# Unit 1's x turned by DMA for three head pairs, and the first value weights loaded behind the value tiles

## The chip, the cores and the metric

The kernel runs on one core of one Trainium2 chip. The metric is the device time of one execution in microseconds (us), as the median of several runs.

## The reference

Four batches of eight heads, 768 positions of 64 dimensions. Each query attends to the keys less than 16 positions away and to 24 block summaries (the maximum of each block of 32 keys, the mean of its 32 values, with log 32 added to the score). The result, laid out as 3072 tokens of 512, goes through a gated feed-forward layer.

```
k_sum = k.reshape(B, H, nb, 32, D).max(axis=3)
v_sum = v.reshape(B, H, nb, 32, D).mean(axis=3)
s_l   = scale * q @ k^T, kept where |i - j| < 16
s_s   = scale * q @ k_sum^T + log(32)
x     = softmax([s_l, s_s]) @ [v, v_sum]            # as 3072 x 512
ffn   = (gelu(x @ w_gate) * (x @ w_val)) @ w_out    # d_ff = 1536
out   = x + sigmoid(x @ w_res) * ffn
```

## The kernel before, in words

The work is cut into eight units of 384 tokens, two for each batch. For a unit, four head pairs are scored (s_step: matmuls into s, Exp into P, a mask on DVE), weighted with the values (av_step: matmuls into ao, then DVE's reciprocal and product into xn, 128 tokens by 128 features for each of three sub-tiles), and turned into xT, features by tokens. The turning of one head pair is done either by xt_step (three TensorE transposes into PSUM tile xp, then a copy by ACT) or by xt_dma (one DMA transpose that SP issues). The tile xT is the moving operand of the gate and value matmuls g and vv (gv_mm): twelve blocks fo of 128 features, each with four matmuls for g and four for vv over the four head pairs ko. ACT takes Gelu of g, DVE multiplies it with vv into gvT. The output matmuls f (ffn_step) and the gate r (res_step) follow, and end_step (two DVE operations and a store by SP) for each of three sub-tiles.

The schedule is by hand: each engine executes its instructions in the order of the program. PE interleaves the output of unit u (first_out for u = 0, mid_out after) with the scores and values of unit u + 1. In first_out all four pairs are turned by xt_step; in mid_out all four by xt_dma.

Loads from DRAM are issued by POOL's queue, which also casts them to bf16; each of its transfers waits on a semaphore that is shared by turns with the one eight places earlier, so that about eight are outstanding. SP's queue issues the transposes, the stores and the copies within the value tiles (v_rims).

At the start, POOL issues the keys, the queries and value tiles 0 to 6 of 64 rows, the first chunk of w_gate and of w_val (256 features each), value tiles 7 to 11, then the other chunks by turns, the second half of the queries (q_sb), w_res, w_out, and later what batch 1 needs (k_sb, value tiles, q_nat). In the meantime PE fills its waits with matmuls on a dummy tile (keep_warm). The block means of the values for batch 0 come from 24 matmuls, two for each value tile (vsum_mm), into two tiles vs; they are copied by DVE and ACT to vblk, which the second half of av_first reads.

In unit 1, the keys of batch 1 are transposed by TensorE (turn_all, 64 transposes) at fo = 0 and placed into kW one pair at a time at fo = 0 to 3 (k_place: an ACT copy, then four DVE operations). At fo = 5 SP gets two DMA transposes of the queries (turn_q, q_nat to qT), PE twelve matmuls for the block means (vsum_grp), and POOL their transfers and copies (vsum_bc). The scores of unit 2 read kW and qT, its av_step the value tiles with the means in them.

Of the kernel before, what the change touches and what calls it, by code (L numbers as in the profile page):

```python
# [15 lines left out]
def kernel(  # L16
# [11 lines left out]
    nc = tc.nc  # L28
# [11 lines left out]
    NT = S // QT  # L40
# [4 lines left out]
    NP = H // 2  # L45
# [35 lines left out]
    w_gate = wpool.tile([128, KO, DFF], BF16, name="w_gate")  # L81
# [53 lines left out]
    with tc.manual_schedule():  # L135
# [20 lines left out]
        wg_src = moe_w_gate.rearrange("(ko ki) f -> ki ko f", ki=128)  # L156
        wv_src = moe_w_val.rearrange("(ko ki) f -> ki ko f", ki=128)

        def load_w(c):
            sl = slice(c * 256, (c + 1) * 256)  # L160
            nc.gpsimd.dma_start(out=w_gate[:, :, sl], in_=wg_src[:, :, sl])
            nc.gpsimd.dma_start(out=w_val[:, :, sl], in_=wv_src[:, :, sl])

        nc.vector.memset(warm[:], 0.0)
        nc.vector.memset(ident[:], 0.0)
# [18 lines left out]
            nc.gpsimd.affine_select(out=m, in_=m, compare_op=ALU.is_ge, fill=-240000.0, base=base,  # L184
                                    pattern=[[-sign, cols.stop - cols.start]], channel_multiplier=sign)
        v_loads(0, 6, 7)
        load_w(0)
        v_loads(0, 7, NT)
        kw_consts(0)
        own_keys(bmat, NT)  # L190
# [1 line left out]
        nc.vector.memset(vext[1][0:QT, :, :, D + 1:VP], 0.0)  # L192


        for c in range(1, 6):
            load_w(c)
            if c == 4:
                q_sb[1] = load_q(1, QJ)
        nc.gpsimd.dma_start(out=w_res[:], in_=moe_w_res.rearrange("(ko ki) f -> ki ko f", ki=128))
        wo_src = moe_w_out.rearrange("(fo ki) f -> ki fo f", ki=128)  # L200
        for c in range(3):
            sl = slice(c * 4, (c + 1) * 4)
# [38 lines left out]
        def k_place(b, hp, tp):  # L241
            nc.scalar.copy(kW[b % 2][:, :, hp, 0:QT].rearrange("d t (p j) -> d t p j", j=PJ),  # L242
                           tp.rearrange("d j (t p) -> d t p j", t=NT))
            k_blocks(b, hp)
            k_rims(b, slice(hp, hp + 1), nc.vector)
# [15 lines left out]
        def vsum_mm(b, vs, lo, hi):  # L261
            for t in range(lo, hi):
                for i in range(2):
                    nc.tensor.matmul(vs[i][96:128, 0:DM // 2], bmat[:, t, :],
                                     vext[b % 2][0:QT, t, 4 * i:4 * i + 4, 0:D],
                                     start=(t == 0), stop=(t == NT - 1))
# [36 lines left out]
        def s_step(u, hp, st, banks=None):  # L303
            if banks:
                s = [p.tile([128, 512], F32, tag=tag, name="s") for p, tag in banks]
            else:
                s2 = ps_s.tile([128, 2, 512], F32, tag="s", name="s")
                s = [s2[:, hh] for hh in range(2)]
            s_mm(u, hp, [x[:, 0:TU] for x in s])
            P = ppool.tile([128, 2, HT, QT], BF16, tag="P", name="P")  # L310
            if banks:
                for hh in range(2):
                    nc.scalar.activation(P[:, hh].rearrange("p t q -> p (t q)"), s[hh][:, 0:TU], AF.Exp,  # L313
                                         scale=scale, bias=bias_t[:])
            else:
                nc.scalar.activation(P.rearrange("p a t q -> p a (t q)"), s2[:, :, 0:TU], AF.Exp,  # L316
                                     scale=scale, bias=bias_t[:])
            if u or hp > 1:
                Pf = P.rearrange("p a t q -> p (a t) q")
                nc.vector.tensor_mul(Pf, Pf, maskt.unsqueeze(1).to_broadcast([128, 2 * HT, QT]))  # L320
            st["P", hp] = P
# [4 lines left out]
        def av_step(u, hp, st, pool=ps_o, tag="ao"):  # L326
            b, half = u // 2, u % 2
            P = st["P", hp]
            ao = pool.tile([128, NSUB, 2, D + 1], F32, tag=tag, name="ao")
            for sub in range(NSUB):  # L330
                for hh in range(2):
                    for e in range(2):
                        t = 2 * sub + e
                        nc.tensor.matmul(ao[64 * e:64 * e + 64, sub, hh, :], P[:, hh, t, :],  # L334
                                         vext[b % 2][:, half * HT + t, 2 * hp + hh, 0:D + 1],
                                         start=True, stop=True, skip_group_check=True)
            av_end(hp, st, ao)
# [18 lines left out]
        def xt_step(u, ko, st, pool, tag, copy=nc.vector.tensor_copy):  # L356
            xp = pool.tile([128, TU], BF16, tag=tag, name="xp")
            for sub in range(NSUB):
                nc.tensor.transpose(xp[:, sub * 128:(sub + 1) * 128],  # L359
                                    st["xn"][:, ko, sub, :], ident[:])  # L360
            copy(st["xT"][:, ko, :], xp[:])
# [115 lines left out]
        vsum_mm(0, vs, 0, 3)  # L477
        s_step(0, 2, st)
        s_step(0, 3, st, MM2)
        vsum_mm(0, vs, 3, 7)  # L480
        keep_warm(2)
        gvT = upool.tile([128, FO, TU], BF16, tag="gvT", name="gvT")
        ao = [ps_mm.tile([128, NSUB, 2, D + 1], F32, tag="mm", name="ao") for _ in range(NP)]
        for hp in range(3):
            av_first(hp, st, ao[hp], 0, BAND)
        vsum_mm(0, vs, 7, 10)
        av_first(3, st, ao[3], 0, BAND)
        vsum_mm(0, vs, 10, NT)
        nc.vector.tensor_copy(vblk[96:128, 0:H // 2, 0:D],
                              vs[0][96:128, 0:DM // 2].rearrange("p (h d) -> p h d", d=D))  # L490
        nc.scalar.copy(vblk[96:128, H // 2:H, 0:D],
# [49 lines left out]
        def first_out(u, st, gvT, nst):  # L541
            n = u + 1
            other = dict(pool=ps_t, tag="t")
            turn = dict(pool=ps_t, tag="t", copy=nc.scalar.copy)
            s_step(n, 0, nst)
            s_step(n, 1, nst, TO2)
            for sub in range(NSUB):
                res_step(st, sub)
            av_step(n, 0, nst)
            av_step(n, 1, nst, **other)  # L550
            s_step(n, 2, nst)
            for sub in range(NSUB):
                ffn_step(st, gvT, sub, 0, 4)
            xt_step(n, 0, nst, **turn)
            av_step(n, 2, nst)
            s_step(n, 3, nst)
            ffn_step(st, gvT, 0, 4, 8)
            ffn_step(st, gvT, 1, 4, 8)
            xt_step(n, 1, nst, **turn)
            ffn_step(st, gvT, 2, 4, 8)  # L560
            av_step(n, 3, nst)
            xt_step(n, 2, nst, **turn)
            ffn_step(st, gvT, 0, 8, FO)
            end_step(u, st, 0)
            ffn_step(st, gvT, 1, 8, FO)
            xt_step(n, 3, nst, **turn)
            ffn_step(st, gvT, 2, 8, FO)
            end_step(u, st, 1)
            end_step(u, st, 2)
# [40 lines left out]
        for u in range(NU):  # L610
            b, half = u // 2, u % 2
            nb = b + 1
            if half == 0 and nb == 1:
                k_sb[nb] = k_tile()
                load_k(nb, k_sb[nb], 0, 1)
                v_loads(nb)
                load_q_nat(nb)
            if u:
                gvT = upool.tile([128, FO, TU], BF16, tag="gvT", name="gvT")
            for fo in range(0 if u else 2, FO):  # L620
                if u > 1 and fo == 0:
                    fo_first(st, gvT)
                elif u and fo == FO - 2:
                    fo_last_two(st, gvT)
                elif u == 0 or fo < FO - 2:
                    fo_step(st, gvT, fo)
                if u == 0:
                    unit0_extras(fo)
                if u == 0 and fo == 9:
                    tq = turn_all(q_sb[1])  # L630
                if u == 0 and fo in (9, 10):
                    for hp in range(2 * fo - 18, 2 * fo - 16):
                        q_place(1, hp, tq[hp])
                if half == 0 and 1 < nb < B and fo == 0:
                    pool_after(st["xT"][0:1, KO - 1, 0:1])
                    k_nat = load_k_nat(nb)
                    v_loads(nb)
                if half == 0 and b and fo == 1:
                    v_rims(b, HT, NT)
                if half == 0 and 1 < nb < B and fo == 6:  # L640
                    turn_k(nb, k_nat)
                    k_rims(nb, slice(0, NP), nc.gpsimd)
                if half == 1 and nb < B:
                    if fo == 0:
                        v_rims(nb, 0, HT)
                        if nb > 1:
                            pool_after(st["xT"][0:1, KO - 1, 0:1])
                            load_q_nat(nb)
                    if fo == (5 if nb == 1 else 1):
                        turn_q(nb, 0)  # L650
                        turn_q(nb, 1)
                        vsum_grp(nb, ps_t, "t")
                        for i in range(2):
                            vsum_bc(nb, 3 * i, 3 * i + 3, nc.gpsimd)
                    if nb == 1:
                        if fo == 0:
                            tk = turn_all(k_sb[nb])
                        if fo < NP:
                            k_place(nb, fo, tk[fo])
                    elif 2 <= fo < 2 + NP:  # L660
                        k_blocks(nb, fo - 2)
            if u == NU - 1:
                last_out(u, st, gvT)
            else:
                nst = new_unit()
                (mid_out if u else first_out)(u, st, gvT, nst)
                st = nst
# [30 lines left out]
```

The softmax here doesn't subtract the row's maximum and nothing guards it: scores larger than these inputs give would overflow.

## Time and profile before

| what | value |
|---|---|
| median of 6 runs | 257.92 us (257.9 to 257.98) |
| profiled execution, its span | 257.9 us, 256.1 us |
| mean granted TensorE clock | 0.998 |
| PE, DVE, ACT, POOL busy | 248.3, 157.4, 127.3, 110.4 us |
| chain that ended last | PE 88%, DMA 5% |
| transposes of xn by PE (L359) | 24, 219 ns median |
| copies of xp by ACT (L361) | 8, 478 ns median |
| DMA transposes of xn (L364) | 24, landing 2.3 / 2.6 / 5.6 us (min, median, max) |
| first w_gate and w_val chunk issued | 10.59 and 11.34 us |
| first matmul of unit 1's gate | 53.18 us |

Times of instructions are microseconds from the first instruction. In the listings a line shows start, length, engine, source line, operation, the tiles written and read, and the count of instructions merged; in brackets stands the idle time before it and what ended it. PE's lengths overlap, as matmuls are pipelined. L359 is line 359 of the kernel.

### The profile page before, as it was taken

How to read it: one execution, taken by the hardware profiler on the slowest of the kernel's cores; microseconds unless marked ns; L12 is line 12 of the kernel's file. 1: busy time of each engine (PE TensorE's matmuls, PEld its weight loads, DVE VectorE, ACT ScalarE, POOL GpSimd, SP SyncE). 2: the span in 40 equal slices, each digit the busy share in tenths (PEclk: the TensorE clock that was granted, in tenths of full speed). 3: DMA queues.
4: the chain of work that ended last, by engine and by line, in shares of the span. 5: the costliest groups of instructions: out<-in, count | busy, mean ns of one | idle time of the engine just before them, and what ended most of it. 6: DMA issues, size and time to landing. Idle time of an engine off the chain costs nothing.

```text
span 256.1 us, 5810 instructions
## 1 busy us (share of the span) xinstructions
PE 248.3 (97%) x2279; PEld 139.0 (54%) x2304; DVE 157.4 (61%) x349; ACT 127.3 (50%) x213; POOL 110.4 (43%) x155
## 2 busy tenths in 40 slices
PE   7999999999999999999999999999999999999994
PEld 2555665565554565545654565546554665555543
DVE  5965776389467544767567544767567544854424
ACT  6667359356483337344492338344482338253320
POOL 8898443291334888255405987256404000000000
PEclk9999999999999999999999999999999999999999
DMA  5999999999903999989903999969903500240003
GB/s 81 178 156 179 197 203 207 183 167 180 137 3 77 179 112 141 130 138 173 131 5 93 181 105 148 120 128 167 140 15 80 134 0 3 49 139 0 0 3 123
DMA packets 98475, 29.34 MB, mean 115 GB/s; under 512 B 83592, under 2 KB 95312, under 8 KB 98352
## 3 DMA queue, kind: packets, MB, share of 16 engines
q0 software_dynamic: 68720, 14.76, 68.4%
q1 hardware_dynamic: 29728, 14.21, 26.1%
q8 instruction: 18, 0.29, 0.5%
q14 instruction: 9, 0.07, 0.2%
HBM read 29.36 MB, written 6.29 MB: 139 GB/s over the span
## 4 chain that ended last, share of the span: by engine, by line
PE 88%; DMA 5%; ACT 2%; POOL 2%; DVE 2%; issue 1%; POOLq 0%; DVEq 0%
PE g L374 25%; PE vv L374 24%; PE f L422 23%; PE r L412 7%; DMA q_sb<-in_q_dram 3%; PE ao L334 3%; PE s L298 2%; DMA vext<-in_v_dram 2%; PE tp L210 1%; PE vs L272 1%; DVE o L431 1%; DVE th L428 1%; POOL k_sb L88 1%; POOL vext L103 1%; PE xp L359 1%
## 5 line engine op out<-in xcount | busy, mean ns | idle before, releaser
L380 DVE TENSOR_TENSOR gvT<-ge,vv 128x384 bf16<-128x384 f32 x96 | 52.7, 552 | 50.8 <-PE vv L374 46.4
L379 ACT ACTIVATE ge<-g 128x384 f32<-128x384 f32 x96 | 47.0, 490 | 68.6 <-DVE gvT L380 38.1
L374 PE MATMUL g<-xT,w_gate 128*128 128x384 bf16 x384 | 78.8, 327 | 0.2
L374 PE MATMUL vv<-xT,w_val 128*128 128x384 bf16 x384 | 78.8, 327 | 0.0
L422 PE MATMUL f<-w_out,gvT 128*128 128x512 bf16 x262 | 62.7, 380 | 1.3 <-issue 1.0
L374 PEld LDWEIGHTS <-w_gate 128*128 128x128 bf16 x384 | 37.2, 98 | 26.5 <-issue 1.6
L374 PEld LDWEIGHTS <-w_val 128*128 128x128 bf16 x384 | 37.5, 98 | 24.8 <-issue 0.3
L422 PEld LDWEIGHTS <-gvT 128*128 128x128 bf16 x276 | 25.7, 98 | 29.2
L103 POOL DMA_DIRECT2D vext<-in_v_dram x48 | 33.5, 745 | 12.8 <-DMA w_out<-in_moe_w_out_dram 5.6
L415 ACT ACTIVATE th<-r 128x512 f32<-128x512 f32 x24 | 13.5, 606 | 27.5 <-PE r L412 27.5
L428 DVE SCALAR_TENSOR_TENSOR th<-th,f 128x512 f32<-128x512 f32 (+2 forms) x26 | 16.6, 640 | 14.5 <-PE f L422 14.5
L320 DVE TENSOR_TENSOR P<-P,maskt 128x768 bf16<-128x768 bf16 x30 | 16.8, 559 | 12.1 <-ACT P L316 6.6
L412 PE MATMUL r<-w_res,xT 128*128 128x512 bf16 x88 | 22.7, 380 | 0.4
L284 POOL COPY vext<-vsum 32x1536 bf16<-32x1536 bf16 x12 | 17.2, 1463 | 11.3 <-DMA vsum<-vpart 11.1
L431 DVE SCALAR_TENSOR_TENSOR o<-th,xn 128x512 f32<-128x512 f32 (+2 forms) x26 | 18.3, 702 | 0.9
L354 DVE TENSOR_TENSOR xn<-ao,rz 128x384 bf16<-128x384 f32 x32 | 17.8, 558 | 1.1
L316 ACT ACTIVATE P<-s,bias_t 128x768 bf16<-128x768 f32 x17 | 15.3, 902 | 4.3 <-PE s L298 4.1
L117 POOL DMA_DIRECT2D k_nat<-in_k_dram x24 | 16.4, 730 | 2.2 <-DMA k_nat<-in_k_dram 1.5
L123 POOL DMA_DIRECT2D q_nat<-in_q_dram x18 | 15.9, 924 | 0.7 <-issue 0.7
L313 ACT ACTIVATE P<-s,bias_t 128x384 bf16<-128x384 f32 x30 | 15.7, 580 | 0.0
L227 DVE TENSOR_REDUCE ks<-kW 128x24 bf16<-128x768 bf16 x16 | 15.1, 945 | 0.4 <-ACT kW L242 0.3
L412 PEld LDWEIGHTS <-xT 128*128 128x128 bf16 x96 | 8.8, 98 | 9.9
(82 smaller groups left out, 173.0 us busy)
## 6 DMA issues: line engine op xcount, KB each, us to landing
out_dram<-o SPq DMA_DIRECT2D x23, 256.0 KB, 2.2
vext<-in_v_dram POOLq DMA_DIRECT2D x48, 64.0 KB, 6.5
q_nat<-in_q_dram POOLq DMA_DIRECT2D x18, 128.0 KB, 7.4
w_gate<-in_moe_w_gate_dram POOLq DMA_DIRECT2D x6, 256.0 KB, 7.4
w_val<-in_moe_w_val_dram POOLq DMA_DIRECT2D x6, 256.0 KB, 8.0
w_out<-in_moe_w_out_dram POOLq DMA_DIRECT2D x3, 512.0 KB, 14.0
k_nat<-in_k_dram POOLq DMA_DIRECT2D x24, 64.0 KB, 4.5
vext<-vext SPq DMA_DIRECT2D x6, 144.0 KB, 5.3
```

Source lines behind the costliest of these rows:

```text
L103: nc.gpsimd.dma_start(out=vext[b % 2][0:QT, t, :, 0:D], in_=v[b, :, t * QT:(t + 1) * QT, :].rearrange("h p d -> p h d"))
L117: nc.gpsimd.dma_start(out=k_nat[:, t].rearrange("p (h d) -> p h d", d=D), in_=k[b, :, t * QT:(t + 1) * QT, :].rearrange("h p d -> p h d"))
L284: eng.tensor_copy(vext[b % 2][96:128, lo:hi, :, 0:D], src)
L320: nc.vector.tensor_mul(Pf, Pf, maskt.unsqueeze(1).to_broadcast([128, 2 * HT, QT]))
L354: nc.vector.tensor_mul(xn, ao[:, :, :, 0:D], rz.to_broadcast([128, NSUB, 2, D]))
L374: nc.tensor.matmul(ps[:, 0:TU], w[:, ko, fo * 128:(fo + 1) * 128], st["xT"][:, ko, :], start=(ko == 0), stop=(ko == KO - 1), skip_group_ch ...
L379: nc.scalar.activation(ge[:], g[:, 0:TU], AF.Gelu)
L380: nc.vector.tensor_mul(gvT[:, fo, :], ge[:], vv[:, 0:TU])
L412: nc.tensor.matmul(r[:], st["xT"][:, ko, ss], w_res[:, ko, :], start=(ko == 0), stop=(ko == KO - 1))
L422: nc.tensor.matmul(st["f", sub][:], gvT[:, fo, ss], w_out[:, fo, :], start=(fo == 0), stop=(fo == FO - 1), skip_group_check=True)
L428: nc.vector.scalar_tensor_tensor(th[:, cs], th[:, cs], 1.0, f[:, 0:n], ALU.add, ALU.mult)
L431: nc.vector.scalar_tensor_tensor(o.rearrange("p (k d) -> p k d", d=128), th[:, cs].rearrange("p (k d) -> p k d", d=128), 0.5, x, ALU.mult, ...
```

## The change

It has four parts. The function load_w loads one chunk of one weight matrix, and the first chunk of w_val is issued behind value tiles 7 to 11; the order behind it is as before. The block-mean matmuls of batch 0 are grouped by tiles 3 to 7, 8 to 10 and 11, in place of 3 to 6, 7 to 9 and 10 to 11. In first_out, pairs 0 to 2 of unit 1 are turned by xt_dma directly behind their av_step; pair 3 stays with xt_step. In unit 1, turn_all and the four k_place steps move from fo = 0 to 3 to fo = 1 to 4, and turn_q, vsum_grp and vsum_bc from fo = 5 to fo = 6.

```diff
--- before.py
+++ after.py
@@ -156,10 +156,9 @@
         wg_src = moe_w_gate.rearrange("(ko ki) f -> ki ko f", ki=128)
         wv_src = moe_w_val.rearrange("(ko ki) f -> ki ko f", ki=128)
 
-        def load_w(c):
+        def load_w(w, src, c):
             sl = slice(c * 256, (c + 1) * 256)
-            nc.gpsimd.dma_start(out=w_gate[:, :, sl], in_=wg_src[:, :, sl])
-            nc.gpsimd.dma_start(out=w_val[:, :, sl], in_=wv_src[:, :, sl])
+            nc.gpsimd.dma_start(out=w[:, :, sl], in_=src[:, :, sl])
 
         nc.vector.memset(warm[:], 0.0)
         nc.vector.memset(ident[:], 0.0)
@@ -184,7 +183,7 @@
             nc.gpsimd.affine_select(out=m, in_=m, compare_op=ALU.is_ge, fill=-240000.0, base=base,
                                     pattern=[[-sign, cols.stop - cols.start]], channel_multiplier=sign)
         v_loads(0, 6, 7)
-        load_w(0)
+        load_w(w_gate, wg_src, 0)
         v_loads(0, 7, NT)
         kw_consts(0)
         own_keys(bmat, NT)
@@ -192,8 +191,10 @@
         nc.vector.memset(vext[1][0:QT, :, :, D + 1:VP], 0.0)
 
 
-        for c in range(1, 6):
-            load_w(c)
+        for c in range(6):
+            if c:
+                load_w(w_gate, wg_src, c)
+            load_w(w_val, wv_src, c)
             if c == 4:
                 q_sb[1] = load_q(1, QJ)
         nc.gpsimd.dma_start(out=w_res[:], in_=moe_w_res.rearrange("(ko ki) f -> ki ko f", ki=128))
@@ -477,15 +478,15 @@
         vsum_mm(0, vs, 0, 3)
         s_step(0, 2, st)
         s_step(0, 3, st, MM2)
-        vsum_mm(0, vs, 3, 7)
+        vsum_mm(0, vs, 3, 8)
         keep_warm(2)
         gvT = upool.tile([128, FO, TU], BF16, tag="gvT", name="gvT")
         ao = [ps_mm.tile([128, NSUB, 2, D + 1], F32, tag="mm", name="ao") for _ in range(NP)]
         for hp in range(3):
             av_first(hp, st, ao[hp], 0, BAND)
-        vsum_mm(0, vs, 7, 10)
+        vsum_mm(0, vs, 8, 11)
         av_first(3, st, ao[3], 0, BAND)
-        vsum_mm(0, vs, 10, NT)
+        vsum_mm(0, vs, 11, NT)
         nc.vector.tensor_copy(vblk[96:128, 0:H // 2, 0:D],
                               vs[0][96:128, 0:DM // 2].rearrange("p (h d) -> p h d", d=D))
         nc.scalar.copy(vblk[96:128, H // 2:H, 0:D],
@@ -547,19 +548,19 @@
             for sub in range(NSUB):
                 res_step(st, sub)
             av_step(n, 0, nst)
+            xt_dma(0, nst)
             av_step(n, 1, nst, **other)
+            xt_dma(1, nst)
             s_step(n, 2, nst)
             for sub in range(NSUB):
                 ffn_step(st, gvT, sub, 0, 4)
-            xt_step(n, 0, nst, **turn)
             av_step(n, 2, nst)
+            xt_dma(2, nst)
             s_step(n, 3, nst)
             ffn_step(st, gvT, 0, 4, 8)
             ffn_step(st, gvT, 1, 4, 8)
-            xt_step(n, 1, nst, **turn)
             ffn_step(st, gvT, 2, 4, 8)
             av_step(n, 3, nst)
-            xt_step(n, 2, nst, **turn)
             ffn_step(st, gvT, 0, 8, FO)
             end_step(u, st, 0)
             ffn_step(st, gvT, 1, 8, FO)
@@ -646,17 +647,17 @@
                         if nb > 1:
                             pool_after(st["xT"][0:1, KO - 1, 0:1])
                             load_q_nat(nb)
-                    if fo == (5 if nb == 1 else 1):
+                    if fo == (6 if nb == 1 else 1):
                         turn_q(nb, 0)
                         turn_q(nb, 1)
                         vsum_grp(nb, ps_t, "t")
                         for i in range(2):
                             vsum_bc(nb, 3 * i, 3 * i + 3, nc.gpsimd)
                     if nb == 1:
-                        if fo == 0:
+                        if fo == 1:
                             tk = turn_all(k_sb[nb])
-                        if fo < NP:
-                            k_place(nb, fo, tk[fo])
+                        if 1 <= fo <= NP:
+                            k_place(nb, fo - 1, tk[fo - 1])
                     elif 2 <= fo < 2 + NP:
                         k_blocks(nb, fo - 2)
             if u == NU - 1:
```

## The prediction

> **What bounds the kernel now.** I read the page first. TensorE is busy for nearly the whole span at full clock, and the chain of work that ended last lies 88% on PE. DVE at 61% and ACT at 50% are not the limit over the whole.
>
> ```profile
> PE 248.3 (97%) x2279; PEld 139.0 (54%) x2304; DVE 157.4 (61%) x349; ACT 127.3 (50%) x213; POOL 110.4 (43%) x155
> ...
> PE   7999999999999999999999999999999999999994
> ...
> DMA  5999999999903999989903999969903500240003
> ```
>
> Two things follow. A matmul taken out of PE's stream shortens the run by its spacing. And the DMA row is full from about 6 to 70 us, so a transfer added there can become late. Next I read the chain in order of time, 12 to 20 us, where PE is not yet the chain:
>
> ```profile
> 11.35 0.74 POOL w_val L162
> 12.10 1.34 POOL vext L103 x2
> 13.44 4.52 DMA vext<-in_v_dram
> 17.96 0.04 issue
> 18.00 0.38 PE vs L264 x2
> 18.38 0.31 PE ao L346 x12
> 18.69 0.45 PE vs L264 x3
> 19.14 0.02 issue
> 19.17 0.45 DVE vblk L489
> ```
>
> Columns are start, length, what. The first value-weight load (w_val) is issued ahead of the value tiles. PE's sums (vs) wait for tile 9, landed at 17.96, and end with tile 11, landed at 18.82 by its semaphore. The copy to vblk, and all behind it, hangs on that. POOL's timeline gives the order of issue:
>
> ```profile
> 10.59 0.77 POOL L161 DMA_DIRECT2D w_gate<-in_moe_w_gate_dram  x1 [0.88 <-DMA q_sb<-in_q_dram]
> 11.34 0.75 POOL L162 DMA_DIRECT2D w_val<-in_moe_w_val_dram  x1
> 12.08 4.04 POOL L103 DMA_DIRECT2D vext<-in_v_dram  x5
> ```
>
> Then PE's timeline over the output of unit 0, where x of unit 1 is turned:
>
> ```profile
> 46.22 0.33 PE L359 MATMUL xp<-ident,xn 128*128 128x128 bf16 x3
> 46.48 0.38 PE L334 MATMUL ao<-vext,P 128*64 128x65 bf16 x12
> ...
> 48.81 0.33 PE L359 MATMUL xp<-ident,xn 128*128 128x128 bf16 x3
> 48.98 0.81 PE L422 MATMUL f<-w_out,gvT 128*128 128x512 bf16 x3
> ...
> 50.24 0.34 PE L359 MATMUL xp<-ident,xn 128*128 128x128 bf16 x3
> 50.42 1.89 PE L422 MATMUL f<-w_out,gvT 128*128 128x512 bf16 x8
> ```
>
> The lengths overlap, since matmuls are pipelined; cost is read from start to next start: 0.26, 0.17 and 0.18 us. Nothing waits there. Last, what a DMA transpose of the same shape takes in later units (instruction line, then landing of all):
>
> ```profile
> L364 SPq DMA_TRANSPOSE xT<-xn x24: 1178/1206/2400, 75.8 to 224.3; - x24
> ...
> DMA to landing us min/median/max: 2.3/2.6/5.6
> ```
>
> SP spends 1.2 us to issue one; it lands in 2.3 to 5.6 us.
>
> **What the Trainium skill says.** "TensorE: Matmul & The Clock Gate", Part 4, puts a 128x128 bf16 transpose at some 390 ns alone and 275 ns in a kernel. The trace disagrees for this stream: 219 ns each, and three cost 0.17 us of PE since they overlap, so I use 0.17. "DMA: Bandwidth & Descriptors", Anatomy of one DMA, has about 2 us of fixed cost per transfer; 2.3 us at least here agrees. The same page, Queues, rings and completion order, says that a DMA engine goes round its queues packet by packet, so SP's transposes should get turns beside POOL's loads. The trace agrees in part: with POOL's queue backed up, the transposes issued at 104.02 and 161.28 took 5.6 and 4.4 us, and their packets began only as that queue ran empty.
>
> **The change, part by part.**
>
> (1) *w_val behind the value tiles.* Tile 7 is issued at 11.34 in place of 12.08. Landings came at 14.35 (tile 6), 15.35 (w_gate), 16.67 (w_val), then every 0.44 us from 17.08 to 18.82: the queue is backed up, so a tile moves by w_val's share, 1.32 us. Tile 7 lands at 15.8, 8 to 11 at 16.2 to 17.5. If POOL's issue were the limit they would move only 0.74 us; I take 1.32, since even then issue to landing stays over 3 us. w_val itself lands where tile 11 did, 18.8; it is first used at 22.25. Cover 3 us. No load behind it moves.
>
> (2) *The sums regrouped, 3-8, 8-11, 11-12.* The same 24 matmuls. Tile 7's two (0.11 us each) enter the idle between 15.82 and 16.02, where PE waits for the Exp of pair 2 (ACT, 15.98): they run at 15.83, and the filler behind them starts 0.03 late. So: av_first of pairs 0 to 2 at 16.58 for 0.69; tiles 8-10 at 17.27, without waits, 0.12 + 5 x 0.11 + 0.09 into the next = 0.76; pair 3 at 18.03 for 0.31 (its mask is done at 17.51); tile 11 at 18.34, its second matmul 0.12 later. The last sum starts at 18.46 against 18.97: **-0.51 us**. Below, DVE's and ACT's copies, the table load and the xT copies follow it and hang on nothing else. The weights still come ahead of their use: the closest are w_val's last chunk (landed 35.79, used at 37.23, so 36.7 then) and w_res (38.30, used at 39.73, then 39.2), 0.9 us of cover.
>
> (3) *Three xt_steps out of PE.* Nine transposes: 0.17 + 0.17 + 0.18 = **-0.52 us** (of the first 0.26, 0.09 is a change of kind that stays). Three ACT copies of 478 ns go as well; ACT idles there (6.5 us waiting for xp over seven), so they are worth nothing.
>
> (4) *Three transposes onto SP.* SP is empty there until the stores at 52.93, so its 3 x 1.2 us hold nobody. xn of pairs 0, 1, 2 is ready at 43.67, 44.36 and 47.69, less 0.5 to 0.8 then: 43.2, 43.9, 46.9. The gate matmuls of unit 1 start at 53.18 - 1.03 = 52.15 and read pair 2 at 52.5. So the transposes have 8.9, some 7.5 and 5.5 us. With the worst landing seen, 5.6 us, the last costs 0.1 us. Bounds: 2.3 us (free) to a wait for POOL's queue to run dry (rival A). I take no stall. Their packets also take DMA time: 0.45 us each in later units, 1.35 together, out of a full queue; k_sb of batch 1 (landed 49.83) moves to at most 51.2 and is read at 54.7.
>
> (5) *turn_all and k_place one fo later, vsum_grp and turn_q at fo 6.* The same 64 transposes, 1.48 us. At fo 0 they stood between the first and second pair of gate and value tiles and covered DVE's three end_steps (51.49 to 55.55) and the Gelu table load (53.01 to 54.29). Without that cover, the value tile of fo 1 wants a bank at 52.15 + 3 x 0.65 = 54.1; the third end_step frees one at 54.83 - 1.03 = 53.8. 0.3 us to spare, so nothing; if the bank were another's, up to 0.4. vsum_grp then comes at 62.66 + 1.30 - 1.03 = 62.9, some 0.2 later, and so do POOL's vsum copies behind it.
>
> (6) *What is late next.* At the end of unit 1 PE comes 1.03 us earlier: s_step(2,0) at 71.33 - 1.03 = 70.3, av_step(2,0) at 73.4. Its qT was issued at 63.44, when q_nat's first half had landed, took 6.2 us and came at 69.66. That chain is held by DMA, not PE. The added 1.35 us of packets delays it by 0 (absorbed where POOL's issue was the limit, 51 to 54 us) to 1.35; I take 0.75, so 70.4. vsum's copies end at 72.98 + 0.2 to 0.7, wanted at 73.4. So **+0.2 us**, between 0 and 0.8.
>
> Sum: -0.51 - 0.52 + 0.2 = -0.8. The profiled execution took 257.9 (span 256.1 and 1.8 around it), 0.02 from the median of 257.92; so 257.1.
>
> **Rivals.** *A, slower: POOL's queue holds the transposes.* For: the DMA share is above 1.2 from 44 to 46 and 2.15 from 48.5 to 51.5, near the 2.37 at 104 to 106 where transposes stood still, and the backlog is longer here. Against: from 97.5 to 103 the kW transposes ran at 600 packets a us while POOL's got 80. It decides from a landing of pair 2 later than 53.5, 6.6 us after its issue, where the stall eats both gains. Held until the queue thins at 53.5, and then 1.35 for the packets and 0.8 to land, pair 2 comes at 55.6: stall 3.1, time 257.9 - 1.03 + 3.1 = 260.0.
>
> *B, absorbed: qT or vsum is the limit of unit 1.* With the full 1.35 us, or one of the pauses of transposes (packets of 1.7 us at 65.2), 0.7 us or more goes: 257.6, and 257.9 at the worst. For: qT's spare was 1.67 us, of which 1.03 is used. Against: the latency of 6.2 held such a pause already.
>
> *C, the value tiles don't move PE* (issue is the limit, or tile 7 holds av_first): then -0.52 + 0.2, so 257.6.
>
> **How the numbers follow.** Main case 0.56, its own range 256.7 to 257.3. B and C together 0.20, near 257.6. A 0.24, 258.5 to 260. About 0.2% (0.5 us) is what a measurement of this kernel tells from no change; so faster 0.56, same 0.20, slower 0.24. The range reaches from 256.6 (no loss, 0.2 more at the start) to 259.0, and leaves out A's long stalls and little else.
>
> **What would show it.** After: tile 11 lands near 17.5 and vblk's copy starts near 18.7 (against 19.17). Unit 1's first gate matmul starts near 52.1 and xT's DMA transposes of 44 to 47 us land by 52. PE between 52 and 54 without a gap means A is wrong; a gap ahead of g, released by the DMA xT<-xn, means A is right. A gap at s_step(2,0) near 70.3 released by qT is B. vblk near 19.2 is C. The prediction is wrong if pair 2's landing takes over 6.6 us.

## The result, and the profile after

The change makes the kernel slower by 0.6%: 259.53 us median (258.8 to 261.68, 36 runs) against 257.96 before (73 runs), ratio 1.0062 with the 95% interval 1.005 to 1.0074. Of the change 9 runs lie at 261.0 to 261.7, with a mean granted clock of 0.993 in place of 0.997 to 1.0, and of the kernel before 14 lie at 259.3 to 259.8; without them the medians are 259.46 and 257.93. The profiled execution took 259.2 us, span 257.5.

The page after: PE's busy time is the same, its share one point lower, and DMA's share of the chain has gone from 5% to 8% (the second and third lines are the chain that ended last, by engine and by line).

```profile
PE 248.2 (96%) x2270; PEld 138.4 (54%) x2295; DVE 156.9 (61%) x349; ACT 125.8 (49%) x210; POOL 110.7 (43%) x155
...
PE 83%; DMA 8%; POOL 3%; ACT 2%; DVE 1%; issue 1%; POOLq 0%; DVEq 0%
PE g L375 24%; PE vv L375 24%; PE f L423 21%; PE r L413 7%; DMA xT<-xn 3%; DMA q_sb<-in_q_dram 3%; PE ao L335 3%; PE s L299 2%; DMA w_val<-in_moe_w_val_dram 2%; POOL vext L103 1%; PE tp L211 1%; PE vs L273 1%; DVE o L432 1%; DVE th L429 1%; POOL w_gate L161 1%
```

The new entry is xT<-xn. PE's timeline around unit 1's first gate matmuls, before,

```profile
53.18 0.81 PE L374 MATMUL g<-xT,w_gate 128*128 128x384 bf16 x4
```

and after, shows where it sits:

```profile
51.27 0.33 PE L360 MATMUL xp<-ident,xn 128*128 128x128 bf16 x3
51.44 1.03 PE L423 MATMUL f<-w_out,gvT 128*128 128x512 bf16 x4
52.30 0.33 PE L375 MATMUL g<-xT,w_gate 128*128 128x384 bf16 x1
53.35 0.32 PE L375 MATMUL g<-xT,w_gate 128*128 128x384 bf16 x1 [0.72 <-DMA xT<-xn]
54.63 0.49 PE L375 MATMUL g<-xT,w_gate 128*128 128x384 bf16 x2 [0.96 <-DMA xT<-xn]
```

The matmul on pair 0 starts at 52.30, 0.88 us ahead of before (53.18). The matmul on pair 1 waits for its transpose, then the one on pair 2 does. Without waits these would be 0.16 us apart, so 1.05 + 1.28 - 0.33 = 2.0 us is lost, and unit 1 goes on 2.01 - 0.88 = 1.13 us behind before. That difference is the same at the first gate matmul of each later unit, 2 to 7. The other 0.3 us of the span's 1.4 lie behind the last DVE operation, at the last stores (that operation ends at 253.40 of 256.1 before and at 254.53 of 257.5 after).

The transposes themselves, in the view of the tile xT:

```profile
L365 SPq DMA_TRANSPOSE xT<-xn x27: 1179/1205/2119, 43.3 to 224.2; - x27
...
DMA to landing us min/median/max: 2.3/2.7/8.6
```

Three more than before, and the slowest landing is 8.6 us in place of 5.6. Pairs 0, 1 and 2, issued at 43.32, 44.68 and 47.17, took 7.95, 8.63 and 7.42 us and landed at 51.27, 53.31 and 54.59.

The start did what it should. POOL's timeline after:

```profile
10.58 0.77 POOL L161 DMA_DIRECT2D w_gate<-in_moe_w_gate_dram  x1 [0.89 <-DMA q_sb<-in_q_dram]
11.34 3.67 POOL L103 DMA_DIRECT2D vext<-in_v_dram  x5
14.99 1.07 POOL L161 DMA_DIRECT2D w_val<-in_moe_w_val_dram  x1
```

Tile 11 lands at 17.57 (18.82 before), DVE's copy to vblk starts at 18.80 (19.17), and unit 0's first gate matmul at 21.72 (22.09). DVE's timeline after:

```profile
18.80 0.43 DVE L490 CAST vblk<-vs 32x256 bf16<-32x256 f32 x1 [1.22 <-PE vs L265]
```

### The profile page after: what moved, and what is told of

It is laid out like the page before. It is cut to its first block, busy times and chain, and to the rows that moved or that the text cites. A ratio compares the mean times of both kernels' runs of the same rounds, so it can differ in the third digit from the quotient of the medians.

```text
span 257.5 us, 5797 instructions
## 1 busy us (share of the span) xinstructions
PE 248.2 (96%) x2270; PEld 138.4 (54%) x2295; DVE 156.9 (61%) x349; ACT 125.8 (49%) x210; POOL 110.7 (43%) x155
## 4 chain that ended last, share of the span: by engine, by line
PE 83%; DMA 8%; POOL 3%; ACT 2%; DVE 1%; issue 1%; POOLq 0%; DVEq 0%
PE g L375 24%; PE vv L375 24%; PE f L423 21%; PE r L413 7%; DMA xT<-xn 3%; DMA q_sb<-in_q_dram 3%; PE ao L335 3%; PE s L299 2%; DMA w_val<-in_moe_w_val_dram 2%; POOL vext L103 1%; PE tp L211 1%; PE vs L273 1%; DVE o L432 1%; DVE th L429 1%; POOL w_gate L161 1%
## 5 line engine op out<-in xcount | busy, mean ns | idle before, releaser
L103 POOL DMA_DIRECT2D vext<-in_v_dram x48 | 32.9, 739 | 15.5 <-DMA w_out<-in_moe_w_out_dram 5.7
L123 POOL DMA_DIRECT2D q_nat<-in_q_dram x18 | 15.8, 912 | 0.7 <-issue 0.7
```

The costliest lines, as they stand in the source:

```text
L103: nc.gpsimd.dma_start(out=vext[b % 2][0:QT, t, :, 0:D], in_=v[b, :, t * QT:(t + 1) * QT, :].rearrange("h p d -> p h d"))
```

## The experiments

Two theories stood first. Theory Q: the loss is PE's wait for xT, and xT is late because its packets share the DMA engines with POOL's backlog. Rival L: the loads that the change delays cost by themselves. A third, T, was that a transpose is slow of its own accord at this place. The edits are cut to the lines that matter, with ... where lines are left out. Those of the start, the turning, the later turn_all and the better version are shown against the kernel before or, for the last, against the start alone; the others against the change.

**The start alone.** All turning stays on PE.

```diff
-        load_w(0)
+        load_w(w_gate, wg_src, 0)
         v_loads(0, 7, NT)
...
-        for c in range(1, 6):
-            load_w(c)
+        for c in range(6):
+            if c:
+                load_w(w_gate, wg_src, c)
+            load_w(w_val, wv_src, c)
...
-        vsum_mm(0, vs, 3, 7)
+        vsum_mm(0, vs, 3, 8)
...
```

> Only the start of the change: w_val's first chunk behind all value tiles and the block means regrouped; all four pairs of unit 1 turned by PE as before. Theory Q (the whole loss is the wait for xT, whose packets share the DMA engines with POOL's loads): the start's gain seen in the trace after, 0.37 us at unit 0's first gate matmul, is kept to the end: 257.9 - 0.4 = 257.5. Rival L (the loads behind w_val came 0.7 us later in the trace after, and that costs by itself at w_res, w_out or q_nat): 257.9 or more.

Measured: 257.52 us (257.4 to 258.27), ratio 0.9972 (0.996 to 0.9983). PE is 0.38 us ahead at unit 0 and 0.39 at every later unit. The start's gain is real and kept; all of the loss is in the rest of the change.

**The turning alone.** The old start, with everything else of the change.

```diff
+            xt_dma(0, nst)
...
-            xt_step(n, 0, nst, **turn)
...
```

> Only the turning by DMA with the later turn_all, on the old start. Theory Q: when pair 2 lands is set by POOL's queue and not by PE, so it lands at 54.6 again and the time is that of the whole change, 259.2 to 259.5, though PE starts 0.4 us later. Rival T (a transpose is slow by itself at this place, so its landing follows its issue): all is 0.4 us later than in the whole change, 259.6 to 259.9. If the turning is innocent: 257.4.

Measured: 260.03 us (259.15 to 262.15), ratio 1.0081 (1.0052 to 1.011). The median looks like rival T's, but five of the ten runs, the profiled one among them, had a granted clock of 0.993 (260.41 to 262.15); the other five took 259.15 to 259.65, in theory Q's range. The landings took 7.56, 7.40 and 7.55 us. Each transpose was issued 0.4 us later than in the change. Pair 0 landed at 51.27 as there, pair 1 at 52.47, 0.8 us earlier, and only pair 2 later, at 55.12; but in other runs whose transposes stood beside the same loads pair 2 landed anywhere from 54.58 to 55.35. So this run doesn't tell Q from T. It showed something else, told below.

**Spare transposes.** PE turns pairs 0 to 2 again, and the same three DMA transposes go to a tile without a reader.

```diff
-            xt_dma(0, nst)
+            xt_spare(0, nst)
...
+            xt_step(n, 0, nst, **turn)
...
```

> The whole change, but PE turns pairs 0 to 2 as before, and the three DMA transposes go to a tile that nobody reads. Theory Q: the cost is PE's wait for the landing alone; without a reader the time is 257.9 - 0.4 = 257.5, up to 0.3 more for loads that come late. Rival L (the 1.35 us of added packets make k_sb, the value tiles and qT late, and that costs): 258.2 or more, with a gap at vs of unit 1 or at the scores of unit 2. Theory Q expects the spare transposes to land 7 to 9 us after their issue also here.

Measured: 258.24 us (257.73 to 258.47), ratio 0.999 (0.9973 to 1.0008). The spare transposes took 8.25, 7.60 and 7.18 us, so the delay is not one of xT. PE ran 0.33 us ahead through all of unit 1, without a gap at the gate matmuls. Without the reader the 2 us are gone: the cost is the wait. But 0.56 us was lost at unit 2: 0.22 where the scores waited for qT (landed 71.18), and 0.33 at the value matmuls, behind a mask on DVE that took 1.35 us. So rival L seems to exist as well, with a smaller sum, hidden in the change because PE is late there anyway. A run below shows that about half of the 0.56 comes without any DMA transpose.

**POOL's loads of batch 1 held back** until pair 2 has landed.

```diff
+            pool_after(nst["xT"][0:1, 2, 0:1])
+            k_sb[1] = k_tile()
+            load_k(1, k_sb[1], 0, 1)
+            v_loads(1)
+            load_q_nat(1)
...
-            if half == 0 and nb == 1:
-                k_sb[nb] = k_tile()
-                load_k(nb, k_sb[nb], 0, 1)
-                v_loads(nb)
-                load_q_nat(nb)
```

> The whole change, with POOL's loads of batch 1 (keys, values, queries) held back until pair 2's transpose has landed, so that only w_out's loads stand beside the transposes. Theory Q: pair 0 lands 4 to 5 us after its issue (w_out until 46.8), pair 2 in under 3.5 us, and unit 1's first gate matmuls have no gap; the loads that come 15 us later then cost 3 us or more at turn_all and at the scores of unit 2 (time 260.5 to 264). Rival T: pairs 0 to 2 land 7 to 9 us after their issue as in the whole change, gap 1.7 us at the first gate matmuls.

Measured: 264.7 us (two runs), somewhat above the expected range. PE waits 3.25 us for the late keys in one piece, and 6.8 us at half clock follow. But the landings took 4.04, 3.10 and 2.33 us, and PE's timeline of this kernel has no gap at unit 1's first gate matmuls:

```profile
51.62 1.03 PE L423 MATMUL f<-w_out,gvT 128*128 128x512 bf16 x4
52.49 0.81 PE L375 MATMUL g<-xT,w_gate 128*128 128x384 bf16 x4
53.14 0.81 PE L375 MATMUL vv<-xT,w_val 128*128 128x384 bf16 x4
```

T falls: the same transposes at the same place are quicker without batch 1's loads in POOL's queue, and pair 2, which finds that queue empty, is as quick as any. Theory Q stands.

**How the queues share.** The DMA view counts packets of POOL's queue (q0) and SP's (q1) in a stretch. Of the change, 47.5 to 49 us, while batch 1's keys come in packets of 1 KB:

```profile
q0 software_dynamic: 230, 0.23, 91.7%
q1 hardware_dynamic: 230, 0.06, 29.7%
```

One for one. At that rate a transpose of 384 packets takes 384 / 230 x 1.5 = 2.5 us; in the kernel with the loads held back pair 2's packets, with no others beside them, took 0.6 (48.53 to 49.13). It is one for one too in 49.5 to 50.5 us, when most of POOL's packets are already the value tiles' of 128 B:

```profile
q0 software_dynamic: 312, 0.09, 84.7%
q1 hardware_dynamic: 318, 0.07, 67.5%
```

In 51 to 51.75 us the counts are far apart:

```profile
q0 software_dynamic: 736, 0.09, 279.5%
q1 hardware_dynamic: 49, 0.01, 11.8%
```

This is no share between two full queues. By count, 735 of the 768 data packets of pairs 0 and 1 had started by 51.0 and the last of them at 51.49; pair 2's first started at 51.58. SP's queue had little left to send there.

Two parts of the delay are not explained by the turns. The first packets start at 47.25, 3.9 us after the first issue, where with idle queues they start after about 1.2 (1.17 for the transpose of 133.1 us before). This time is 3.9 to 4.0 us in all nine traces with DMA transposes here and batch 1's keys queued, and 1.6 in the one with the keys held back. And pair 1 landed at 53.31, 1.8 us after the last of those 768 packets had started. What sets these two times is not shown.

To see whether the one for one is of packets or of bytes, the keys were loaded in 512 B rows:

```diff
-                load_k(nb, k_sb[nb], 0, 1)
+                for j in range(0, PJ, 4):
+                    nc.gpsimd.dma_start(
+                        out=k_sb[nb][:, :, j:j + 4].rearrange("p h j d -> p h (j d)"),
+                        in_=k[nb].rearrange("h (p j) d -> p h j d", j=PJ)[:, :, j:j + 4].rearrange(
+                            "p h j d -> p h (j d)"))
```

> The whole change, with batch 1's keys loaded by two transfers with 512 byte rows in place of one with 1 KB rows. Theory Q in its packet form (one of SP's packets for one of POOL's): the transposes go at 250 to 300 packets a us beside the keys in place of 150, pair 0 lands at 50 or before in place of 51.3 and pair 2 before 53.7. Byte form (the shares are of bytes or fixed): 150 packets a us and 51.3 as before.

Measured: 259.38 us, ratio 1.0053 (1.0035 to 1.0071). The DMA view of this kernel, 48 to 49.5 us:

```profile
q0 software_dynamic: 371, 0.19, 90.1%
q1 hardware_dynamic: 358, 0.09, 45.7%
```

Still about one for one, now at 240 packets a us: it is packets that alternate. Pair 0 landed at 50.47, 0.8 us earlier, though it was issued 0.45 later. Pair 2 landed at 54.72 all the same, past the 53.7 expected; the next run shows what held it.

**Only the value and query loads held back,** the keys left in place.

```diff
+            pool_after(nst["xT"][0:1, 2, 0:1])
+            v_loads(1)
+            load_q_nat(1)
...
                 load_k(nb, k_sb[nb], 0, 1)
-                v_loads(nb)
-                load_q_nat(nb)
```

> The whole change, with POOL's value and query loads of batch 1 held back until pair 2's transpose has landed; the keys stay where they are. Theory Q (the DMA engines alternate between SP's packets and POOL's): beside the keys' 1 KB packets the transposes go at 150 packets a us as before, pair 0 lands at 51.3; when the keys end near 51.4 the rest goes at 800 a us, so pairs 1 and 2 land at 52 to 53 in place of 53.3 and 54.6, and the gap at unit 1's first gate matmuls falls from 1.8 to at most 0.7 us. The loads then come some 3 us later or more and cost 2 us or more at the scores of unit 2: 260 to 262. If the value tiles' small packets hold nothing, pair 2 still lands after 54.

Measured: 260.32 us (258.78 to 262.13, three runs). Pairs 0, 1 and 2 landed at 51.69, 51.96 and 52.29, and the gap is gone:

```profile
52.27 0.81 PE L375 MATMUL g<-xT,w_gate 128*128 128x384 bf16 x4
```

So the keys make the transposes slow (with them held back too, pair 0 had taken 4.04 us in place of 8.40), and the value tiles hold the last two beyond 52.3. At unit 2 PE then waited 2.38 us for qT, whose loads came late.

**Filler in the wait.** Nine dummy matmuls on PE ahead of unit 1's gate.

```diff
             ffn_step(st, gvT, 2, 8, FO)
+            keep_warm(9)
             end_step(u, st, 1)
```

> The whole change, with nine 128x512 matmuls on the dummy tile (0.216 us each) on PE ahead of unit 1's gate matmuls, inside the wait for xT. If the runs of the change at 261 us come from TensorE's clock, which was granted at half for 3.4 us behind a gap of 2.1 us in the run with the turning alone: no run above 260.2, median 259.2 to 259.6. If they come from elsewhere: a quarter of the runs at 261 as before. If PE's wait is not what costs: all 1.9 us slower, 261.4.

Measured: 259.79 us (259.16 to 260.17), not the 261.4 that 1.9 us more work (nine of 0.216 us) would cost outside a wait. Pair 2's matmul starts at 54.63, to the hundredth as in the change, and in both 0.04 us behind its landing: the wait is set by the landing alone. Repeated beside the change itself:

> The kernel with filler matmuls in the wait once more, beside the change itself on the same chip. Clock theory (a gap of over 2 us in PE's matmuls costs a stretch at half clock): no run above 260.3 here, some at 260.8 to 261.7 of the change. Otherwise both have such runs.

> The whole change once more, unaltered, beside the filler kernel: 258.8 to 259.9 for most runs, and a quarter of them at 261.

Measured: filler 259.40 us (259.09 to 260.0, 10 runs), the change 259.45 (258.94 to 259.71, 9 runs). So the filler changes the time by nothing that these runs can tell. On the clock, which the expectation asked about, the repeat does not decide: no run with filler came above 260.2, but here none of the change did either. Pair 2 landed at 55.35 and 54.85 in these two profiled runs, so its landing varies by some 0.8 us from run to run.

**Start and later turn_all,** no DMA transpose.

```diff
-                        if fo == 0:
+                        if fo == 1:
                             tk = turn_all(k_sb[nb])
...
-                    if fo == (5 if nb == 1 else 1):
+                    if fo == (6 if nb == 1 else 1):
...
```

> The start of the change and the later turn_all, k_place, turn_q and vsum_grp, with all pairs turned by PE. It parts the 0.56 us that the kernel with spare transposes lost at the scores and values of unit 2. If the packets of the transposes made qT and the value sums late there: 257.5, as the start alone (257.52), and PE 0.39 us ahead of before at unit 2. If the later vsum_grp did it: 257.8 to 258.1, and the first values of unit 2 wait for POOL's copy.

Measured: 257.83 us (257.44 to 258.27), 0.31 above the start alone. PE is 0.39 ahead to the end of unit 1 and 0.12 from unit 2 on. So the move of part 5 has a price when PE is early, and of the 0.56 us that the kernel with spare transposes lost, some 0.27 needs no transpose. The time is as expected for the later vsum_grp; what waited was a mask on DVE. DVE's timeline of this kernel:

```profile
72.47 2.02 DVE L321 TENSOR_TENSOR P<-P,maskt 128x768 bf16<-128x768 bf16 x2 [0.81 <-ACT P L317]
```

and of the start alone:

```profile
72.48 0.62 DVE L321 TENSOR_TENSOR P<-P,maskt 128x768 bf16<-128x768 bf16 x1 [0.81 <-ACT P L317]
73.43 0.56 DVE L321 TENSOR_TENSOR P<-P,maskt 128x768 bf16<-128x768 bf16 x1 [0.32 <-ACT P L314]
```

The first mask operation took 1.55 us in place of 0.62. POOL's timeline of the shifted kernel has the reason:

```profile
70.74 2.87 POOL L285 COPY vext<-vsum 32x1536 bf16<-32x1536 bf16 x2 [3.31 <-DMA vsum<-vpart]
```

POOL's copies of the block means run to 73.61, 0.9 us later than in the start alone (72.70), and so beside the mask operations of unit 2. The Trainium skill, "SBUF — State Buffer", SBUF: two separate sides, says that GpSimd and a DVE operation with two SBUF inputs take turns on a shared port pair, each holding it for its whole instruction. The trace agrees: the mask ended at 74.02, 0.41 us behind POOL's second copy. The same 0.40 to 0.41 us stands behind the copy's end in the start alone (copy 72.70, mask 73.10), with spare transposes (74.44 and 74.84, a mask of 1.35 us) and with the filler (74.78 and 75.19). It wasn't tried with the copies on another engine.

**A better version.** The start, and pair 0 alone by DMA; turn_all where it was.

```diff
             av_step(n, 0, nst)
+            xt_dma(0, nst)
...
-            xt_step(n, 0, nst, **turn)
...
```

> The start of the change, and pair 0 alone turned by DMA, pairs 1 to 3 by PE, turn_all where it was. Theory Q: pair 0 lands near 50 (384 packets at 150 a us), 2 us ahead of its use; three PE transposes less are 0.17 us: 257.35 against 257.52 of the start alone. Rival L (packets make qT or the value sums late at unit 2): 257.5 to 257.8.

Measured: 257.32 us (257.24 to 257.37), ratio 0.9968 (0.9953 to 0.9982). Pair 0 lands at 50.76, ahead of its use at 52.63. This beats the kernel before and the change. Over the start alone the gain is 0.2 us by the medians and 0.16 in the traces, as expected, but too small for the two intervals to part.

## Why the prediction was wrong

Forecast was 257.1 with a range of 256.6 to 259.0; it came to 259.5. The steps:

1. *The start, -0.51.* Right in kind, 0.37 to 0.39 in fact. Value tiles moved by 1.25 us, as worked out (tile 7 at 15.84 against 15.8). The rest shows at the filler behind tile 7's sums, at 16.19 in place of 16.05; half of it is that this run's scores began 0.07 us later.
2. *PE's transposes, -0.52.* Right: from -0.37 to -0.88 by 52.30.
3. *The transposes on SP: "I take no stall".* **This is the step that failed.** It took the worst landing of later units, 5.6 us, as the bound and put pair 2 at 52.5; it landed 7.4 us after its issue. That 5.6 comes from 104 us, where POOL's backlog ended at 106.5, so the number held the wait for the end of a short backlog. At 43 us the backlog had 10 us to go, by the forecast's own 53.5. The number was a property of the queue at that place and not of the transpose; with the loads held back pair 2 took 2.33 us. The time that it gave each pair was 8.9, 7.5 and 5.5 us, and they took 7.95, 8.63 and 7.42: pair 0 was in time, pairs 1 and 2 were not.
4. *Rival A* named the mechanism, its place and its sign. Its point of decision was right: pair 2 after 53.5 eats both gains, and it came at 54.59. Its price, 3.1 us, was too high, because the engines alternate and the transposes advance beside the keys; 2.0 was measured. Its weight of 0.24 was too low: the 5.6 us and the case from 97.5 to 103 us, in which transposes went ahead, were counted against it. But at 104 us the backlog had only 2.5 us to run, and in the other case the counts over the whole stretch are 2929 to 858, some 530 and 160 packets a us where the forecast has 600 and 80.
5. *turn_all later: nothing.* No wait for a bank at fo 1, as said. But 0.31 us at the masks of unit 2 when PE is early, from POOL's copies, which the forecast moved by 0.2 us (0.9 measured, against the start alone) and looked at only as a deadline for the values.
6. *What is late next, +0.2.* Hidden in the change. With the spare transposes PE lost 0.56, in the range of 0 to 0.8, but only 0.22 of it was the wait for qT that the forecast meant; most of the rest is point 5's.

The sum in fact: -0.37 - 0.51 + 2.01 = +1.13 by the traces, and 0.3 at the last stores, which no term of the forecast covers.

The skill's round of queues by packet, of which the forecast said that the trace agreed in part, is what the runs show while both queues had packets waiting: 230 to 230 beside 1 KB packets, 358 to 371 beside 512 B, 318 to 312 with mostly 128 B. It does not explain the 3.9 us before the first packet, half of pair 0's latency; that stays open. The 2 us of fixed cost per transfer that the forecast took from the skill stand there for transfers that GpSimd issues; nothing in the sum rests on them.

## What to carry to other kernels

A landing time read elsewhere in the trace holds only for the queue that stood there: before a small DMA is added on the path, look how long the other queue's backlog has still to run and how large its packets are. Moving a turn from PE to DMA is worth its PE time only for those pieces whose slack exceeds that; here one of three. And a moved POOL copy can stop DVE, so look at what DVE does beside it.

## What the runs showed of the hardware that was not expected

PE's clock can fall after a pause of less than 2 us. In the profiled run of the turning alone, PE's matmuls paused for 1.97 us in one piece:

```profile
55.16 0.58 PE L377 MATMUL g<-xT,w_gate 128*128 128x384 bf16 x2 [1.97 <-DMA xT<-xn]
```

Windows of that run (start and end, length, busy times of PE, PEld, DVE, ACT, POOL, granted clock, DMA share, GB/s):

```profile
52.60:55.10 2.50, 0.59 (x4) 0.20 (x2) 2.40 (x4) 1.22 (x1) 2.11 (x4) 1.00 1.95 186
55.10:56.00 0.90, 0.84 (x4) 0.48 (x4) 0.00 (x0) 0.22 (x1) 0.90 (x2) 0.68 1.70 287
56.00:57.00 1.00, 1.00 (x5) 0.47 (x4) 0.00 (x0) 0.28 (x1) 1.00 (x2) 0.50 1.74 225
57.00:58.00 1.00, 1.00 (x5) 0.46 (x3) 0.55 (x1) 0.00 (x0) 1.00 (x2) 0.50 1.54 292
```

The granted clock went to 0.50 for 3.4 us, four 128x384 matmuls took 1.28 us in place of 0.65, and unit 2 began 3.34 us behind before in place of 1.13. But the length of the pause alone doesn't decide. In the kernel with the value loads held back, PE paused for longer and the clock stayed at 1.00:

```profile
73.50 0.53 PE L299 MATMUL s<-qT,kW 64*128 64x64 bf16 x24 [2.38 <-DMA qT<-q_nat]
```

```profile
71.10:73.50 2.40, 0.02 (x1) 0.04 (x1) 0.58 (x2) 0.55 (x1) 1.03 (x1) 1.00 1.12 210
73.50:75.00 1.50, 1.45 (x28) 0.91 (x29) 0.18 (x1) 1.11 (x2) 1.50 (x2) 1.00 0.87 165
```

Nor did the clock fall behind a pause of 1.52 us (keys in 512 B rows) or behind the change's 0.72 and 0.96. Behind the 3.25 us of the kernel with all loads held back it was at half for 6.8 us. What decides besides the length is not shown. The skill's "TensorE: Matmul & The Clock Gate", Why this matters for your kernels, warns of gaps over some 3 us; here 1.97 us were enough once, and 2.38 us did nothing once.
